# One DMA transpose for two halves of an output block, and a new order for the last pair of products, in a two-layer MLP kernel

## Chip, cores, metric

One core of a Trainium2 chip. The metric is device microseconds (us) of the core, lower is better. Times inside a trace count from the start of its span; the device time is 1.7 to 2.1 us longer than the span.

## The reference

```python
B, S, D, F = 1, 2048, 1024, 3584          # x: bf16 (B,S,D); w1 (D,F); w2 (F,D)
def reference(x, w1, b1, w2, b2):
    y = _layernorm(x, axis=-1)
    h = _gelu(jnp.einsum("bsd,df->bsf", y, w1) + b1)
    return jnp.einsum("bsf,fd->bsd", h, w2) + b2
```

## The kernel before

Both layers are matrix products of the Strassen-Winograd kind, in two levels: seven outer products `p`, each of seven inner products `q`. The second layer computes the output transposed (columns on the partitions), so nearly every output block must be turned before it is stored. A block is 512 tokens by 256 columns, and it comes in two halves `dt` of 128 columns. Blocks of one product are named 11, 12, 21, 22.

A small planner inside the kernel lists all work as tasks, packs the on-chip memory (with a seed), simulates the schedule and emits each engine's instructions in the simulated order. Two things follow. Each engine, and each DMA issue queue, has a fixed list that it works off in order: in the trace of this kernel a weight load leaves at 304.74 us, right behind an output store that had waited until 304.32. And any change of sizes or of the seed packs the memory anew and can reorder instructions far away from the edit.

The parts that matter:

```python
UNIT_LA, IN_LA = (6, 5), 5          # how many products ahead a weight unit is asked for
SEED = 4
# order of the last two outer products: digits are q and dt; "p" marks the outer product before the last
END_ORDER = "11 10 p41 p40 51 p31 61 50 p30 71 60 31 70 30 20 40 41 21"

def finish(dt, i, k, u, v, a, na, bb, nb, name, alone=False, q="SP"):
    o = M.alloc(1024, "o")
    ...
    op("DVE", ..., tensor_tensor(out=o, in0=a, in1=bb, op=add), ...)
    if key not in OT:
        OT[key] = M.alloc(2048, "ot")
    t = OT[key]
    half = view[:, :, dt * P:(dt + 1) * P]
    dma("SP", dma_start_transpose(half, o), ...)         # one transpose per half
    if alone:                store(... half ...)
    elif len(t.cells) == 2:  store(... both halves ...)

def last_ends(dt):           # dt = 1 only: blocks 11 and 21 come "by tokens"
    def turn(u, src, cell):  # the sum so far is split into two fp16 parts, turned by DMA, added again
        ...
        dma("SP", dma_start_transpose(tt, hl), ...)
    def end(u, q):           # last inner product with tokens on the partitions: needs no turn
        prod2(dt, 3)(q, bank, True, tiles)
        op("DVE", ..., add) ; store(...)
...
# a weight load may leave once the product just before the place UNIT_LA places earlier is done (gate)
put(i - (UNIT_LA[0] if p == P_ORDER[0] else UNIT_LA[1]), lambda p=p, q=q: w2_unit(p, q))
```

## Time and profile before

| | before |
|---|---|
| device time, three runs | 338.09 us median (337.15 to 339.26) |
| span of the traced run | 336.6 us |
| tensor engine busy | 327.4 us |
| last matmul ends | 330.43 us |
| tail from there to the end | 6.17 us |
| DMA transposes | 44 (12 of the input, 30 of block halves, 2 double ones of the last blocks) |

The tensor engine is the bound, so the kernel can win only in the few microseconds in which that engine does nothing, or does work that is not needed. Read the view of its waits for the gaps, the end of the chain of waits for the tail, and the timeline with the issue queues (SPq is the sync queue, ACTq the scalar queue) for what fills the tail. The lines stand in the prediction below.

### The profile page before, as it was taken

What the parts mean: (1) busy time and instruction counts of PE and PEld (TensorE: products, weight loads), DVE (VectorE), ACT (ScalarE), POOL (GpSimd) and SP (SyncE); (2) the same over time, 40 slices, a digit from 0 to 9 for tenths busy, and PEclk for the clock granted to TensorE, in tenths of its full rate; (3) what the DMA queues carried; (4) which work ended last, traced back from release to release, by engine and by line L of the source; (5) the groups of instructions that cost most, each with busy time, mean ns of one, the idle gap of its engine ahead of it and who ended that gap; (6) DMA issues with size and microseconds to landing.
All of it is one profiled execution on the core that took longest, in us unless ns stands there. A gap on an engine that the chain in (4) does not pass through costs nothing.

```text
span 336.6 us, 4741 instructions
## 1 busy us (share of the span) xinstructions
PE 327.4 (97%) x1684; PEld 154.7 (46%) x1684; DVE 299.7 (89%) x488; ACT 181.1 (54%) x309; POOL 14.1 (4%) x28
## 2 busy tenths in 40 slices
PE   8999999999999999999999999999999999998992
PEld 6844444444444444444444444444444444443452
DVE  5979999999989969976969998999999998899782
ACT  4697999998776776768666453542112123121220
POOL 2210021103000000000000000000000000000000
PEclk9999999999999999999999999999999999999997
DMA  6998999999997999998775535556799549999998
GB/s 217 322 239 191 277 242 360 237 321 268 291 344 252 344 324 328 340 343 258 238 218 171 164 115 161 163 157 154 213 229 266 151 135 230 190 250 247 283 213 177
DMA packets 122721, 81.00 MB, mean 241 GB/s; under 512 B 36682, under 2 KB 114122, under 8 KB 122698
## 3 DMA queue, kind: packets, MB, share of 16 engines
q1 hardware_dynamic: 119642, 79.59, 87.2%
q10 hardware_dynamic: 3056, 1.11, 1.4%
q8 instruction: 13, 0.21, 0.3%
q14 instruction: 10, 0.08, 0.1%
HBM read 48.70 MB, written 24.38 MB: 217 GB/s over the span
## 4 chain that ended last, share of the span: by engine, by line
PE 88%; DMA 5%; ACT 2%; SPq 1%; DVE 1%; issue 0%; POOLq 0%; POOL 0%
PE ps L921 43%; PE ps L1242 42%; DMA mem<-in_w_dram 3%; PE ps L1315 2%; DMA mem<-w_raw 2%; PE ps L1249 1%; ACT mem L653 1%; ACT mem L826 1%; DVE mem L782 1%; SPq L771 1%; POOLq L571 0%; ACT mem L842 0%; PE ps L704 0%; SPq L643 0%; ACT mem L650 0%
## 5 line engine op out<-in xcount | busy, mean ns | idle before, releaser
L921 PE MATMUL ps<-mem 128*128 128x512 f16 x756 | 164.3, 379 | 0.5 <-DVE mem L782 0.4
L1242 PE MATMUL ps<-mem 128*128 128x512 f16 x672 | 145.9, 379 | 1.2 <-DMA mem<-w_raw 1.2
L921 PEld LDWEIGHTS ps<-mem 128*128 128x128 f16 (+1 forms) x756 | 73.4, 98 | 90.5 <-DVE mem L782 1.5
L842 ACT COPY mem<-ps 128x512 f32<-128x512 f32 x111 | 64.6, 588 | 77.5 <-PE ps L1242 63.7
L1242 PEld LDWEIGHTS ps<-mem 128*128 128x128 f16 (+1 forms) x672 | 65.7, 98 | 80.7 <-DMA mem<-w_raw 1.7
L826 ACT ACTIVATE mem<-ps,b_sb 128x512 f16<-128x512 f32 x112 | 73.5, 692 | 20.7 <-PE ps L921 13.6
L850 DVE TENSOR_TENSOR ps<-ps,mem 128x512 f32<-128x512 f32 x84 | 58.2, 697 | 13.1 <-ACT mem L842 12.2
L1078 DVE TENSOR_TENSOR mem<-mem 128x2048 f16<-128x2048 f16 (+1 forms) x56 | 59.6, 1087 | 2.1 <-PE ps L1242 1.6
L782 DVE TENSOR_TENSOR mem<-mem 128x1024 f16<-128x1024 bf16 (+1 forms) x56 | 37.9, 688 | 2.8 <-DMA mem<-in_w_dram 2.4
L987 DVE TENSOR_TENSOR mem<-mem 128x512 f16<-128x512 f16 (+5 forms) x84 | 37.0, 465 | 1.2 <-DMA mem<-in_w_dram 0.7
L1090 DVE TENSOR_TENSOR mem<-mem 128x2048 f16<-128x2048 f16 (+1 forms) x32 | 33.4, 1089 | 0.0
L833 ACT COPY ps<-ps 128x512 f32<-128x512 f32 x31 | 17.7, 570 | 24.4 <-DVE mem L1139 15.1
L1111 DVE TENSOR_TENSOR mem<-ps,mem 128x512 bf16<-128x512 f32 x22 | 15.0, 688 | 3.3 <-PE ps L1242 3.2
L971 DVE TENSOR_TENSOR mem<-mem 128x2048 f16<-128x2048 bf16 (+1 forms) x16 | 17.4, 1087 | 0.1
L1139 DVE TENSOR_TENSOR mem<-ps,mem 128x512 f32<-128x512 f32 x24 | 16.4, 687 | 1.2 <-PE ps L1242 1.1
L668 DVE BATCH_NORM_STATS2 st_sb<-mem 128x6 f32<-128x512 bf16 x22 | 14.2, 682 | 3.6 <-DMA mem<-in_x_dram 3.6
L748 DVE TENSOR_TENSOR mem<-mem 128x512 f16<-128x512 f16 x32 | 11.9, 419 | 0.2
L674 POOL TENSOR_TENSOR rstd_sb<-vpe_sb,nhalf 128x1 f32<-128x1 f32 x11 | 7.1, 643 | 50.9 <-DVE vpe_sb L671 50.9
L1273 PE MATMUL ps<-ones 128*128 128x128 bf16 (+1 forms) x55 | 6.8, 292 | 1.1 <-POOL ones L609 1.1
L1315 PE MATMUL ps<-mem 128*128 128x128 f16 x112 | 7.4, 219 | 0.3 <-DMA mem<-in_w_dram 0.2
L1228 ACT COPY ps<-b_sb 128x512 f32<-128x512 f32 x6 | 3.5, 590 | 7.4 <-DVE mem L1139 7.2
L677 DVE TENSOR_SCALAR mem<-mem,mv_sb,rstd_sb 128x1024 f16<-128x1024 bf16 (+1 forms) x12 | 6.2, 520 | 1.4 <-POOL rstd_sb L674 1.3
(40 smaller groups left out, 77.4 us busy)
## 6 DMA issues: line engine op xcount, KB each, us to landing
mem<-in_w_dram SPq DMA_DIRECT2D x80, 256.0 KB, 5.0
mem<-w_scr SPq DMA_DIRECT2D x28, 448.0 KB, 3.7
w_scr<-mem SPq DMA_DIRECT2D x21, 512.0 KB, 5.2
w_raw<-mem SPq DMA_DIRECT2D x12, 512.0 KB, 5.6
mem<-w_raw SPq DMA_DIRECT2D x12, 448.0 KB, 3.9
mem<-in_w_dram SPq DMA_DIRECT2D x9, 448.0 KB, 3.8
mem<-in_x_dram SPq DMA_DIRECT2D x15, 256.0 KB, 4.3
out_dram<-mem SPq DMA_DIRECT2D x12, 256.0 KB, 3.4
```

The costliest lines, as they stand in the source:

```text
L782: op("DVE", d_tt(n), lambda e: e.tensor_tensor(out=o[0], in0=a[0], in1=bb[0], op=f), r=[a[1], bb[1]], w=[o[1]], name=f"w1S{k}_{ch}")
L826: op("ACT", A_GELU, lambda e: e.activation(out=dst, in_=banks[bank][:, :], func=ACT.Gelu_apprx_tanh, bias=b1_sb[:, f:f + 1], scale=1.0), r ...
L833: op("ACT", A_CP, lambda e: e.copy(out=banks[dst][:, :], in_=banks[src][:, :]), r=[bank_c[src]], w=[bank_c[dst]], name=name, lat=A_LAT)
L842: op("ACT", A_CP, lambda e: e.copy(out=v16(a, 0, 2048, F32), in_=banks[src][:, :]), r=[bank_c[src]], w=[a.c()], name=name, lat=A_LAT)
L850: op("DVE", D_PS, lambda e: e.tensor_tensor(out=banks[dst][:, :], in0=banks[src][:, :], in1=v16(a, 0, 2048, F32), op=ALU.add), r=[bank_c[s ...
L921: i = e.matmul(banks[bank][:, :], lhsT=lv[:, k, :], rhs=rv[:, k, :], start=(fresh and k == 0), stop=(k == KH - 1), skip_group_check=True)
L971: op("DVE", d_tt(2 * self.n), lambda e: e.tensor_tensor(out=vd, in0=va, in1=vb, op=ALU.subtract), r=self.cells(a) + self.cells(bb), w=self ...
L987: tt = lambda o, a, c: (lambda e: e.tensor_tensor(out=o, in0=a, in1=c, op=ALU.subtract))
L1078: op("DVE", d_tt((k1 - k0) * 512), lambda e, a=a, bb=bb, o=o: e.tensor_tensor(out=o, in0=a[0], in1=bb[0], op=f), r=a[1] + bb[1], w=[t.c(z) ...
L1090: op("DVE", d_tt((k1 - k0) * 512), lambda e, va=va, vb=vb, vd=vd: e.tensor_tensor(out=vd, in0=va, in1=vb, op=f), r=h_cells(b, a, s, k0, k1 ...
L1139: op("DVE", D_PS, lambda e: e.tensor_tensor(out=av(dst), in0=banks[bank][:, :], in1=av(src), op=ALU.add), r=[bank_c[bank], src.c()], w=[ds ...
L1242: i = e.matmul(banks[bank][:, :], lhsT=bv[:, k, :], rhs=av3[:, k, :], start=(fresh and k == 0), stop=(k == KQ - 1), skip_group_check=True)
```

## The change

Intent: fewer and larger transposes on the sync queue, and no transpose late enough to hold up the end. Both halves of a block go into one tile, so that one transpose turns both. In the last pair, blocks 11 of both halves come last, by tokens. Blocks 21, the ones before, are turned by the tensor engine. Weight units of the late products are asked for earlier. The packing seed is another.

```diff
-UNIT_LA, IN_LA = (6, 5), 5
+UNIT_LA, IN_LA = (6, 5, 5, 6, 7, 10, 12), 5
-SEED = 4
+SEED = 2
-END_ORDER = "11 10 p41 p40 51 p31 61 50 p30 71 60 31 70 30 20 40 41 21"
+FIN_DUE, END_DUE = 12.0, 4.0
+END_ORDER = "11 10 p41 50 p40 p31 61 p30 71 60 51 70 30 31 40 41 t3 20 t7 21"
+END_HOW = {(0, 1, 0): "PE", (1, 1, 0): "PE"}
@@ class Wino
-                    elif not self.copied:
+                    elif not self.copied and q in (2, 6):
@@ finish
+                o = M.alloc(2048 if how == "both" else 1024, "o") if new else OT[key]
+                dst = v16(o, 0, 2048, BF16).rearrange("p (t s c) -> p s t c", t=4, s=2)[:, dt] ...
+                if how == "both" and new:
+                    OT[key] = o
+                elif how == "PE":
+                    turned.append((o, o.c(dt), lambda view, cells: store(...)))
+                else:
+                    dma("SP", lambda e: e.dma_start_transpose(v3(t, 0, t.n, n, BF16), v16(o, 0, o.n, BF16)), ...)
+                    store(..., q=q)
@@ new: the turn by the tensor engine ("t3", "t7" in the order)
+            def turn_pe(bank):
+                    for t in range(4):
+                        r = e.transpose(out=pv[:, t, :], in_=v16(o, t * 256, 256, BF16), identity=id16[:, :])
+                op("ACT", 0.45, lambda e: e.copy(out=view, in_=pv), ...)
+                put_out(view, [t.c()])
@@ last_end: now once per half, for block 11 only
-            groups[last].part, groups[last].end = last_ends(1)
+            for g, into in zip(c_seq[-2:], ((0,), (2, 6))):
+                groups[g].part, groups[g].end = last_end(g[1], into)
... (the planner's own estimates of issue times, the identity, bookkeeping: cut)
```

More of the change, by code (lines that the diff above doesn't have):

```diff
@@ L397, in _simulate @@
                     if e in ("SP", "ACTQ", "POOLQ"):
-                        issue = {"Td": 2.0, "To": 1.0}.get(t.name[:2], DMA_ISSUE)
+                        issue = {"Td": 1.6, "To": 1.5}.get(t.name[:2], DMA_ISSUE)
                         free[h] = now + issue
@@ L525 @@
 TE_DUE = 5.0
-FIN_DUE = 12.0
-END_ORDER = "11 10 p41 p40 51 p31 61 50 p30 71 60 31 70 30 20 40 41 21"
+FIN_DUE, END_DUE = 12.0, 4.0
+END_ORDER = "11 10 p41 50 p40 p31 61 p30 71 60 51 70 30 31 40 41 t3 20 t7 21"
+END_HOW = {(0, 1, 0): "PE", (1, 1, 0): "PE"}
 OPA = {1: "A11", 2: "A12", 3: "S4", 4: "A22", 5: "S1", 6: "S2", 7: "S3"}
@@ L582, in bass_standalone__mixer_channel_mlp__prompt_kernel @@
         identb = sb("identb", [NBR, NBR], BF16)
+        id16 = sb("id16", [P, P], BF16)
         NT = ST // P
@@ L615, in build @@
                r=[c_ones], w=[c_idb], name="identb")
+            c_id16 = Cell()
             op("POOL", 0.2, lambda e: e.memset(nhalf[:, :], -0.5), w=[c_nh], name="nhalf")
@@ L873, in step @@
                         if self.last:
-                            self.part["11"](X)
+                            self.part(X)
                     if q == 1:
@@ L877, in step @@
                     elif q == 2 and self.last:
-                        self.end["11"](((Z + 4) % 8, Z))
+                        self.end()
                     elif q == 2:
@@ L902, in step @@
                         add(Z, Z, self.s3, n + "V")
-                        if self.last:
-                            self.part["21"](self.s3)
                         MA.free(self.s3)
                         self.sink["22"](Z)
-                    if q == 4 and self.last:
-                        self.end["21"]((X,))
-                    elif q == 4:
+                    if q == 4:
                         self.prod(4, Y, False)
@@ L1103, in build @@
             OT = {}
-            def finish(dt, i, k, u, v, a, na, bb, nb, name, alone=False, q="SP"):
-                o = M.alloc(1024, "o")
-                wait = 1.0 if q == "ACTQ" else FIN_DUE
-                pr.due = (pr.last_pe, wait)
-                op("DVE", D_PS, lambda e: e.tensor_tensor(out=v16(o, 0, 1024, BF16), in0=a, in1=bb, op=ALU.add),
-                   r=[na, nb], w=[o.c()], name=name, lat=D_PS_LAT)
-                key = (i, k, u, v)
-                if key not in OT:
-                    OT[key] = M.alloc(2048, "ot")
-                t = OT[key]
-                view = v16(t, 0, 2048, BF16).rearrange("p (t c) -> p t c", t=4)
-                half = view[:, :, dt * P:(dt + 1) * P]
-                pr.due = (pr.last_pe, wait + 5.0)
-                dma("SP", lambda e: e.dma_start_transpose(half, v16(o, 0, 1024, BF16)), [o.c()], [t.c(dt)], P * 1024 * 1.3, None, f"To{key}")
-                pr.due = None
-                M.free(o)
-                if alone:
-                    store(i, k, u, v, half, [t.c(dt)], dt * P, P, q=q)
-                    M.free(OT.pop(key))
-                elif len(t.cells) == 2:
-                    store(i, k, u, v, view, [t.c(0), t.c(1)], 0, 2 * P, q=q)
-                    M.free(OT.pop(key))
@@ new lines, in finish @@
+            def finish(dt, i, k, u, v, a, na, bb, nb, name, how="both", q="SP"):
+                key = (i, k, u, v)
+                pr.due = (pr.last_pe, END_DUE if q == "ACTQ" else FIN_DUE)
+                new = key not in OT or how != "both"
+                o = M.alloc(2048 if how == "both" else 1024, "o") if new else OT[key]
+                dst = v16(o, 0, 2048, BF16).rearrange("p (t s c) -> p s t c", t=4, s=2)[:, dt] if how == "both" else \
+                    v16(o, 0, 1024, BF16).rearrange("p (t c) -> p t c", t=4)
+                four = lambda z: z.rearrange("p (t c) -> p t c", t=4)
+                op("DVE", D_PS, lambda e: e.tensor_tensor(out=dst, in0=four(a), in1=four(bb), op=ALU.add), r=[na, nb], w=[o.c(dt)], name=name,
+                   lat=D_PS_LAT)
+                if how == "both" and new:
+                    OT[key] = o
+                elif how == "PE":
+                    turned.append((o, o.c(dt), lambda view, cells: store(i, k, u, v, view, cells, dt * P, P, q=q)))
+                else:
+                    if how == "both":
+                        OT.pop(key)
+                    n = o.n // 256
+                    pr.due = (pr.last_pe, (END_DUE if q == "ACTQ" else FIN_DUE) + 5.0)
+                    t = M.alloc(o.n, "ot")
+                    dma("SP", lambda e: e.dma_start_transpose(v3(t, 0, t.n, n, BF16), v16(o, 0, o.n, BF16)),
+                        [o.c(0), o.c(1)] if how == "both" else [o.c(dt)], [t.c()], P * o.n * 2.2, None, f"To{i}{k}{u}{v}")
+                    M.free(o)
+                    store(i, k, u, v, v3(t, 0, t.n, 4, BF16), [t.c()], 0 if how == "both" else dt * P, 2 * P if how == "both" else P, q=q)
+                    M.free(t)
+                pr.due = None
@@ new lines, in build, with tr @@
+            turned = []
+            def turn_pe(bank):
+                o, cell, put_out = turned.pop(0)
+                pv = banks[bank][:, :].bitcast(BF16)[:, 0:512].rearrange("p (t c) -> p t c", t=4)
+                def tr(e):
+                    for t in range(4):
+                        r = e.transpose(out=pv[:, t, :], in_=v16(o, t * 256, 256, BF16), identity=id16[:, :])
+                    return r
+                op("PE", 4 * MM128, tr, r=[cell, c_id16], w=[bank_c[bank]], name="turn", lat=PE_LAT)
+                M.free(o)
+                t = M.alloc(1024, "ot")
+                view = v3(t, 0, 1024, 4, BF16)
+                op("ACT", 0.45, lambda e: e.copy(out=view, in_=pv), r=[bank_c[bank]], w=[t.c()], name="turned", lat=A_LAT)
+                put_out(view, [t.c()])
+                M.free(t)
@@ L1167, in f @@
                             e6 = E.pop(("6", k))
-                            finish(dt, 0, 1, u, v, banks[bank][:, :], bank_c[bank], av(e6), e6.c(), n, alone=v == 0,
-                                   q="ACTQ")
+                            finish(dt, 0, 1, u, v, banks[bank][:, :], bank_c[bank], av(e6), e6.c(), n, END_HOW.get((dt, u, v), "both"), "ACTQ")
                             M.free(e6)
@@ L1172, in outer_sink, with last_end, part @@
                 return {"11": mk(0, 0), "12": mk(0, 1), "21": mk(1, 0), "22": mk(1, 1)}
-            def last_ends(dt):
-                nat = {}
-                def turn(u, src, cell):
-                    e6 = E.pop(("6", (dt, u, 0)))
-                    n = f"oe{u}"
-                    op("DVE", D_PS, lambda e: e.tensor_tensor(out=av(e6), in0=src, in1=av(e6), op=ALU.add), r=[cell, e6.c()], w=[e6.c()],
-                       name=n + "a", lat=D_PS_LAT)
+            def last_end(dt, into):
+                ee = []
+                def part(bank):
+                    e6 = E.pop(("6", (dt, 0, 0)))
+                    n = f"oe{dt}"
+                    pr.due = (pr.last_pe, 3.0)
+                    op("DVE", D_PS, lambda e: e.tensor_tensor(out=av(e6), in0=banks[bank][:, :], in1=av(e6), op=ALU.add),
+                       r=[bank_c[bank], e6.c()], w=[e6.c(), bank_c[bank]], name=n + "a", lat=D_PS_LAT)
                     hl = M.alloc(2048, "hl")
@@ L1186, in turn @@
                     op("ACT", A_CP, lambda e: e.copy(out=hi, in_=av(e6)), r=[e6.c()], w=[hl.c(0)], name=n + "h", lat=A_LAT)
-                    op("DVE", D_PS, lambda e: e.tensor_tensor(out=lo, in0=av(e6), in1=hi, op=ALU.subtract), r=[e6.c(), hl.c(0)], w=[hl.c(1)],
-                       name=n + "l", lat=D_PS_LAT)
+                    op("DVE", D_PS, lambda e: e.tensor_tensor(out=lo, in0=av(e6), in1=hi, op=ALU.subtract), r=[e6.c(), hl.c(0)],
+                       w=[hl.c(1)], name=n + "l", lat=D_PS_LAT)
@@ L1189, in turn @@
                     M.free(e6)
                     tt = M.alloc(2048, "tt")
-                    dma("SP", lambda e: e.dma_start_transpose(v3(tt, 0, 2048, 8), v16(hl)), [hl.c(0), hl.c(1)], [tt.c()], P * 2048 * 1.3, None,
-                        f"Td{n}")
+                    pr.due = (pr.last_pe, 8.0)
+                    dma("SP", lambda e: e.dma_start_transpose(v3(tt, 0, 2048, 8), v16(hl)), [hl.c(0), hl.c(1)], [tt.c()], P * 2048 * 2.2,
+                        None, f"Td{n}")
+                    pr.due = None
@@ L1193, in turn @@
                     M.free(hl)
-                    ee = nat[u] = M.alloc(2048, "acc")
-                    op("DVE", D_PS, lambda e: e.tensor_tensor(out=av(ee), in0=v16(tt, 0, 1024), in1=v16(tt, 1024, 1024), op=ALU.add),
-                       r=[tt.c()], w=[ee.c()], name=n + "s")
+                    ee.append(M.alloc(2048, "acc"))
+                    op("DVE", D_PS, lambda e: e.tensor_tensor(out=av(ee[0]), in0=v16(tt, 0, 1024), in1=v16(tt, 1024, 1024), op=ALU.add),
+                       r=[tt.c()], w=[ee[0].c()], name=n + "s")
@@ L1197, in turn @@
                     M.free(tt)
-                def end(u, q):
-                    def f(into):
-                        ee = nat.pop(u)
-                        nt = 4 // len(into)
-                        w = nt * P
-                        for z, bank in enumerate(into):
-                            prod2(dt, 3)(q, bank, True, range(z * nt, (z + 1) * nt))
-                            pr.due = (pr.last_pe, 2.0)
-                            o = M.alloc(2 * w, "o")
-                            a, bb, oo = banks[bank][:, 0:w], av(ee)[:, z * w:(z + 1) * w], v16(o, 0, 2 * w, BF16)
-                            op("DVE", 0.08 + w / 960, lambda e, a=a, bb=bb, oo=oo: e.tensor_tensor(out=oo, in0=a, in1=bb, op=ALU.add),
-                               r=[bank_c[bank], ee.c()], w=[o.c()], name=f"oe{u}_{z}", lat=D_PS_LAT)
-                            store(0, 1, u, 0, oo.rearrange("p (t c) -> p t c", t=nt), [o.c()], dt * P, P, z * nt, nt,
-                                  "ACTQ" if z == 0 else "SP")
-                            pr.due = None
-                            M.free(o)
-                        M.free(ee)
-                    return f
@@ L1217, in last_ends, with end @@
-                part = {"11": lambda bank: turn(0, banks[bank][:, :], bank_c[bank]), "21": lambda a: turn(1, av(a), a.c())}
-                return part, {"11": end(0, 2), "21": end(1, 4)}
+                def end():
+                    nt = 4 // len(into)
+                    w = nt * P
+                    for z, bank in enumerate(into):
+                        prod2(dt, 3)(2, bank, True, range(z * nt, (z + 1) * nt))
+                        pr.due = (pr.last_pe, 2.0)
+                        o = M.alloc(2 * w, "o")
+                        a, bb, oo = banks[bank][:, 0:w], av(ee[0])[:, z * w:(z + 1) * w], v16(o, 0, 2 * w, BF16)
+                        op("DVE", 0.08 + w / 960, lambda e, a=a, bb=bb, oo=oo: e.tensor_tensor(out=oo, in0=a, in1=bb, op=ALU.add),
+                           r=[bank_c[bank], ee[0].c()], w=[o.c()], name=f"oe{dt}_{z}", lat=D_PS_LAT)
+                        store(0, 1, 0, 0, oo.rearrange("p (t c) -> p t c", t=nt), [o.c()], dt * P, P, z * nt, nt,
+                              "ACTQ" if dt == 0 or z == 0 else "SP")
+                        pr.due = None
+                        M.free(o)
+                    M.free(ee[0])
@@ L1220, in b2_seeds @@
+                return part, end
             def b2_seeds(dt, h):
@@ L1389, in build @@
                 flat += both(p, 1) + both(prev, 4) + both(p, 5) + both(prev, 3) + both(p, 2, 6, 7)
-            prev, p, last = P_ORDER[-2], P_ORDER[-1], c_seq[-1]
+            prev, p = P_ORDER[-2], P_ORDER[-1]
             for name in END_ORDER.split():
+                if name[0] == "t":
+                    flat.append(((), int(name[1])))
+                    continue
                 flat.append((("c", int(name[-1]), {"p": prev}.get(name[0], p)), int(name[-2])))
@@ L1437, in build @@
                 for q, (dct, key) in {2: (y, (b, 0)), 3: (y, (b, 1)), 4: (T, (b, 4)), 5: (T, (b, 1)), 6: (T, (b, 2))}.items():
-                    put(max(i for i, (gg, qq) in enumerate(flat) if gg[0] == b and qq == q) + 1,
+                    put(max(i for i, (gg, qq) in enumerate(flat) if gg[:1] == (b,) and qq == q) + 1,
                         lambda dct=dct, key=key: M.free(dct.pop(key)))
@@ L1447, in build @@
                 spread([due(f, DUE_W) for f in W2Sums(k0, k1).steps()], pos(lo), pos(hi))
-            lb = {p: max(i for i, (g, q) in enumerate(flat) if g[0] == "c" and g[2] == p and q in (1, 2, 4)) for p in P_ORDER}
+            lb = {p: max(i for i, (g, q) in enumerate(flat) if g[:1] == ("c",) and g[2] == p and q in (1, 2, 4)) for p in P_ORDER}
             put(fC + S1_AT, lambda: out_sum(0, "S1", "A21", "A22", ALU.add, None))
@@ L1466, in build @@
             for i, (g, q) in enumerate(flat):
-                if g[0] != "c" or i > first_use(g[:1] + (1 - g[1],) + g[2:], (q,)):
+                if g[:1] != ("c",) or i > first_use(g[:1] + (1 - g[1],) + g[2:], (q,)):
                     continue
                 p = g[2]
-                put(i - (UNIT_LA[0] if p == P_ORDER[0] else UNIT_LA[1]), lambda p=p, q=q: w2_unit(p, q))
+                put(i - (UNIT_LA[P_ORDER.index(p)]), lambda p=p, q=q: w2_unit(p, q))
                 if q in (5, 6, 7, 3):
@@ L1479, in build @@
             put(fC - 12, b2_diff)
+            put(fC, lambda: op("POOL", 0.35, lambda e: e.affine_select(out=id16[:, :], in_=ones[:, :], pattern=[[-1, P]],
+                                                                       compare_op=ALU.is_equal, fill=0.0, base=0, channel_multiplier=1),
+                               r=[c_ones], w=[c_id16], name="id16"))
             groups = dict(g1)
@@ L1487, in build @@
                 groups[g] = group2(g[1], g[2], g[1])
-            groups[last].last = True
-            groups[last].part, groups[last].end = last_ends(1)
+            for g, into in zip(c_seq[-2:], ((0,), (2, 6))):
+                groups[g].last = True
+                groups[g].part, groups[g].end = last_end(g[1], into)
             for i, (g, q) in enumerate(flat):
@@ L1494, in build @@
                 gate[0] = None
-                groups[g].step(q)
+                if g:
+                    groups[g].step(q)
+                else:
+                    turn_pe(q)
             for i in sorted(at):
```

## The prediction

> **What bounds the kernel now.** I read the page first (who is busy), then the chain of waits, then the waits of the tensor engine, and last the timeline of the final 35 us with both DMA issue queues in it. All times are us from the start of the span.
>
> The page, parts 1 and 5:
>
> ```profile
> span 336.6 us, 4741 instructions
> PE 327.4 (97%) x1684; PEld 154.7 (46%) x1684; DVE 299.7 (89%) x488; ACT 181.1 (54%) x309; POOL 14.1 (4%) x28
> ...
> L1242 PE MATMUL ps<-mem 128*128 128x512 f16 x672 | 145.9, 379 | 1.2 <-DMA mem<-w_raw 1.2
> ```
>
> The tensor engine is busy for 327.4 of 336.6 us, so whatever the change does elsewhere, only about 9.2 us are not matrix work. The next views say where those 9.2 lie. The waits of the tensor engine alone:
>
> ```profile
> PE ps L1242 <- DMA mem<-w_raw: 1.2, 1, 1.2
> PE ps L1273 <- POOL ones L609: 1.1, 1, 1.1
> PE ps L921 <- DVE mem L782: 0.4, 1, 0.4
> PE ps L1315 <- DMA mem<-in_w_dram: 0.2, 1, 0.2
> ```
>
> That is 2.9 us: 1.3 at the head, 0.4 in the first layer, 1.2 late in the second. What is left is after the last matmul. The chain of waits ends so:
>
> ```profile
> 304.74 5.71 DMA mem<-w_raw
> 310.45 0.05 issue
> 310.50 16.79 PE ps L1242 x77
> 327.29 3.14 PE ps L1249 x56
> 330.43 0.02 issue
> 330.45 0.42 DVE mem L1209
> ```
>
> The reader is to see two things: one weight load of 5.71 us that the tensor engine waited for, and a last matmul at 330.43, so a tail of 336.6 - 330.43 = 6.17 us. The timeline of the two stretches shows why. First around the late load:
>
> ```profile
> 301.94 0.50 SPq L1034 DMA_DIRECT2D mem<-w_scr  x1
> 304.32 0.38 SPq L1100 DMA_DIRECT2D out_dram<-mem  x1
> 304.74 0.51 SPq L1031 DMA_DIRECT2D mem<-w_raw  x1
> ```
>
> The sync queue sat from 302.44 to 304.32 in front of an output store. The sync queue's own list of waits puts this kind of store down to waiting for a transpose to land (8 times, up to 1.8 us). The weight load stands right behind it in the same queue; it was issued at 304.74, landed at 310.45, and the matrix engine had run dry at about 309.32. Then the tail:
>
> ```profile
> 326.30 5.29 SPq L1120 DMA_TRANSPOSE mem<-mem  x4
> ...
> 328.88 5.57 ACTq L1100 DMA_DIRECT2D out_dram<-mem  x6
> ...
> 331.64 0.93 SPq L1100 DMA_DIRECT2D out_dram<-mem  x1
> ```
>
> Four transposes leave back to back, 1.32 us each, and with the two before them the queue is full from 323.51 to 331.59. The store of the last product is ready at 330.45 + 0.42 = 330.87 but leaves at 331.64. Later still, the last of the six stores on the scalar queue leaves at 334.06 (a narrower window shows it alone), because it waits for the transpose issued at 330.32; it lands 2.0 us after its issue, at 336.1, and 0.5 us later the span ends. So the last 6 us are set by the sync queue's transposes, not by the last product.
>
> **What the Trainium skill says.** "DMA: Bandwidth & Descriptors", section "Anatomy of one DMA", says that the DMA engines never wait on a semaphore; the wait is done by the issuing sequencer before dispatch. The trace agrees: the load at 304.74 leaves only after the store at 304.32. The same page, section "DMA Transpose (X-bar)", says that two transpose streams from different queues in flight at once can corrupt each other, so all turns stay on one queue, and it names the tensor engine with an identity as the other way. The trace has all 44 DMA transposes on the sync queue. "TensorE: Matmul & The Clock Gate", section "Wait — 56ns, not 53.3ns?", gives 215.7 and 55.6 ns start to start at 512 and 128 columns; the chain has 119.31 us for 553 wide matmuls (215.7 ns) and 3.14 for 56 narrow ones (56.1 ns), which agrees. No page that I found states what a transpose costs to issue; I use the trace.
>
> **The change part by part.**
>
> 1. Merging the two halves of a block. Before there are 30 block transposes (128 x 512 elements) of 1.24 us median issue and 3.9 us to landing. After it, blocks of the four earlier kinds need one each instead of two (24 become 12), and of the last product two merged ones remain of six, so 14. In the trace a transpose of twice the width costs hardly more to issue: the two double ones near the end took 1.23 and 1.49 us, and landed after 5.7 and 3.7 us. Saved: 16 x 1.24 = 20 us of the sync queue, and nearly none of it on the path by itself. No vector work is saved: the adds stay, with another output layout.
>
> 2. Weight units of the last two products are asked for 10 and 12 products ahead, not 5. One product is 7 matmuls, 1.51 us. The late load's gate so comes 5 x 1.51 = 7.5 us earlier, against a lateness of 1.18 us. I count the whole gap as gone: -1.18.
>
> 3. Both "11" blocks are now the two by tokens at the end (28 narrow matmuls each). Before it was 11 and 21 of one half. So the count of token work is the same, 56 x 0.056 = 3.14 us, and the wide products stay 16. Nothing gained, nothing lost: 0.
>
> 4. Both "21" blocks are turned by the tensor engine, 4 transposes each between the last products: 8 x 0.056 = +0.45 on the tensor engine, if the vector engine's add is done in time. The first is asked for after another product of 1.51 us; the add needs some 0.25 + 0.69, so it is. The scalar engine's two copies of about 0.5 us lie where it has nothing else.
>
> 5. The tail. With parts 2 and 4 the last matmul ends at 330.43 - 1.18 + 0.45 = 329.70. The last half block needs 0.02 + 0.42 for the add, then a store. The sync queue has no transposes left by then (the last, of blocks 12, comes after a product that ends some 6.6 us before the end), so it leaves at 330.2. A store of 64 KB lands 3.3 us after issue on this queue before; then 0.5 to the end: 334.0. The tail is then 4.3 instead of 6.17: -1.85.
>
> Against that the merged transpose of blocks 12: the product ends at about 323.05, add to 324.1, transpose landed at 4.7 us (median of the two double ones) 328.8, store landing 3.1 later, 331.9; at 5.7 us it would be 332.9. Both are before 333.5, so the last product sets the end, with 0.6 to 1.6 us to spare.
>
> Sum: -1.18 + 0.45 - 1.85 = -2.6. The memory is packed anew (another seed, larger output tiles, longer prefetch), and that draws the small waits of 20 to 310 us anew. Before has only 0.4 of them beside the one removed, which is nearly as good as it gets, so I put +0.5 there, a judgement and not a reading. Result -2.1: span 334.5, time 338.09 - 2.1 = 336.0.
>
> **The rivals.**
>
> - A new wait takes the place of the old one. For: the weight units stay allocated longer, the packing is another, and each load is issued in order on one queue; the vector engine is at 100% from 300 to 310.5 already, so a late sum has nowhere to go. Against: the DMA share from 180 to 300 us is 51 to 81%, with room. It would cost 1 to 2 us: 337 to 338.
> - The tail stays set by a DMA. For: a merged transpose starts only when its later half is there, and stores on the scalar queue are in order behind the one that waits for it, with the turned copies on the same engine. Against: the 0.6 to 1.6 us of slack above. It would give back about 1: 337.
> - The turn stalls the tensor engine. For: product, add, turn, copy is a chain over three engines, and the vector engine's order is fixed beforehand; each turn could wait 0.5 to 0.8. Then +1 to +1.5: 337 to 337.5.
> - The gain is larger because the sync queue of the whole second layer is relieved. Against: the tensor engine has no other wait from 95.25 on, so there is nothing to gain there.
>
> **Range and chances.** If all goes as computed without the allowance, 335.5; with one rival whole, 337 to 337.5; with two, 338. The three runs before spread from 337.15 to 339.26, so a median can be off by some 0.5. I take 336.0, and 334.4 to 337.9 for 8 in 10. Faster by over 2% would need 331.3, that is 6.8 us of at most 9.2 that are not matrix work, of which a store's landing alone is 3.3: chance 0.02. Slower by over 2% would need a new stall of 9 us: 0.02. Within 2%: 0.96.
>
> **What would show each step right or wrong.** Part 1: 28 transposes in all instead of 44, the merged at about 1.25 us of issue (wrong if it is near 2.5). Part 2: no wait of the tensor engine for a weight load after 180 us; any there is the first rival. Part 4: 8 narrow transposes on the tensor engine, no idle time before them. Part 5: from the last matmul to the end 4.3 us, and the last store on the sync queue within 0.2 us of the last add; if a store on the scalar queue lands last, the second rival holds. The prediction is wrong as a whole if the busy time of the tensor engine grows by more than 0.5 us or its idle time between 20 and 310 us exceeds 1.5.

## The result

| | before | after |
|---|---|---|
| device time, six runs each on one chip | 337.67 us median (336.74 to 339.26) | 333.88 us median (333.2 to 334.65) |
| ratio, with 95% interval | | 0.9887 (0.9859 to 0.9914) |
| span of the traced run | 336.6 us | 332.7 us |
| last matmul ends | 330.43 us | 329.63 us |
| tail | 6.17 us | 3.07 us |

A ratio is the mean time of one kernel's fast runs over that of the other's fast runs of the same rounds, so it is not quite the ratio of the medians. The change is faster by 1.1%, within the 2% that I gave 0.96, but the time lies 0.5 us below my range. Fewer transposes were issued: 28, of which the 14 output ones took a median of 1.27 us to issue and 4.4 to land.

The page of the changed kernel, parts 1 and 5:

```profile
span 332.7 us, 4721 instructions
PE 328.1 (99%) x1692; PEld 156.2 (47%) x1692; DVE 299.3 (90%) x488; ACT 181.8 (55%) x311; POOL 13.6 (4%) x29
...
L1262 PE MATMUL ps<-mem 128*128 128x512 f16 x672 | 145.7, 379 | 0.0
```

The tensor engine does a little more work than before (328.1 against 327.4) and yet the span is 3.9 us shorter, so all of the gain is idle time (of the 0.7 us more, 2 x 0.22 are the turns shown below, and 0.2 lie in the first 20 us, 18.84 against 18.64 busy); the second layer's wait of 1.2 is now 0.0. The waits of the tensor engine (what waited, for what: us in total, times, longest):

```profile
PE ps L1293 <- POOL ones L611: 1.1, 1, 1.1
PE ps L920 <- DVE mem L751: 0.4, 1, 0.4
```

The late weight load is gone from the list. The granted clock is no rival: its mean was 0.994 in the trace before and 1.000 after, but before it stands at 1.00 until 332 us and falls (to 0.72, then 0.50) only after the last matmul. The end of the chain of waits (start, us, what):

```profile
326.04 0.22 PE ps L1142 x4
326.26 1.56 PE ps L1269 x28
327.83 0.22 PE ps L1142 x4
328.05 1.58 PE ps L1269 x28
329.63 0.02 issue
329.65 0.42 DVE mem L1231
```

The turns on the tensor engine (L1142) cost 2 x 0.22 us with no idle time before them, as worked out beforehand, and the last matmul ends at 329.63 where the prediction had 329.70. (That it fits to 0.07 us is partly luck: in a second trace of the same kernel, after_again below, it ends at 328.93.) Then the issue queues of the tail; the last line is from a narrower window, which shows the second of the two stores alone:

```profile
317.10 7.91 SPq L1126 DMA_TRANSPOSE mem<-mem  x3
325.05 5.43 SPq L1099 DMA_DIRECT2D out_dram<-mem  x2
...
330.10 0.37 SPq L1099 DMA_DIRECT2D out_dram<-mem  x1
```

The last transpose has left by 325.01, and the last store leaves at 330.10, 0.03 us after the last add (329.65 + 0.42). Before it stood 0.77 us behind transposes. The span then ends 2.60 us after that issue.

That is where the prediction breaks: it allowed 3.3 + 0.5 = 3.8 us for this last piece. The DMA view of the last microseconds (how many, KB each, median us from issue to landing), before:

```profile
out_dram<-mem ACTq DMA_DIRECT2D x3, 128.0 KB, 3.1
...
out_dram<-mem ACTq DMA_DIRECT2D x1, 64.0 KB, 3.5
out_dram<-mem SPq DMA_DIRECT2D x1, 64.0 KB, 3.3
```

and after:

```profile
out_dram<-mem ACTq DMA_DIRECT2D x3, 128.0 KB, 2.3
out_dram<-mem ACTq DMA_DIRECT2D x1, 64.0 KB, 1.8
```

The same stores land 0.8 to 1.7 us sooner. For the very last store of the changed kernel the view gives no landing; the 2.60 us to the end bound it. So the view does not show whether this store or the scalar queue's last one (issued at 329.75, landed after 2.2) came in last.

### The profile page after: what moved, and what is told of

It is laid out like the page before. It is cut to its first block, busy times and chain, and to the rows that moved or that the text cites. A ratio compares the mean times of both kernels' runs of the same rounds, so it can differ in the third digit from the quotient of the medians.

```text
span 332.7 us, 4721 instructions
## 1 busy us (share of the span) xinstructions
PE 328.1 (99%) x1692; PEld 156.2 (47%) x1692; DVE 299.3 (90%) x488; ACT 181.8 (55%) x311; POOL 13.6 (4%) x29
## 4 chain that ended last, share of the span: by engine, by line
PE 90%; SPq 5%; DMA 4%; DVE 0%; issue 0%
PE ps L920 45%; PE ps L1262 44%; SPq L774 3%; DMA mem<-mem 2%; DMA mem<-in_w_dram 1%; SPq L646 1%; PE ps L1269 1%; DVE mem L751 0%; SPq L1310 0%; PE ps L1142 0%; DVE mem L1231 0%; SPq L643 0%; SPq L1311 0%
## 5 line engine op out<-in xcount | busy, mean ns | idle before, releaser
L1293 PE MATMUL ps<-ones 128*128 128x128 bf16 (+1 forms) x55 | 7.7, 322 | 1.1 <-POOL ones L611 1.1
L653 ACT ACTIVATE mem<-mem 128x1024 f16<-128x1024 bf16 x5 | 5.3, 1069 | 3.6 <-DMA mem<-in_x_dram 3.6
```

## The experiments

Theory A: the gain is two separate things, a late weight load (1.2 us) and a shorter tail (3.1 us), less 0.45 us of turning. Inside the tail, theory F: stores land late because transposes load the DMA engines. The rivals: B, everything comes from a crowded sync queue; C and H, the new packing of the memory; D, merging does not pay by itself.

The last matmul, the tail and the waits are of the traced run, the rest of the timed runs. A tail is good to some 0.05 us, since the span is read to 0.1. "Weight wait" is the wait of the tensor engine for a second-layer weight load; "other waits" are those of 0.4 us or more after the first microseconds.

| run | last matmul | tail | weight wait | other waits | median us | ratio to before (95%) |
|---|---|---|---|---|---|---|
| before_look1 | 329.52 | 6.28 | 0.7 | none | (337.58) | |
| before_look2 | 330.23 | 5.97 | 1.1 | 0.5 | (337.91) | |
| after_again | 328.93 | 2.97 | none | none | 333.54 | 0.9896 (0.9871 to 0.9921) |
| e1_prefetch_only | 329.17 | 5.53 | none | 0.4 | 336.97 | 1.0003 (0.9976 to 1.0030) |
| e2_merge_only | 328.08 | 7.22 | none | none | 337.78 | 1.0016 (0.9998 to 1.0034) |
| e3_after_old_prefetch | 329.89 | 3.61 | none | 0.6 | 336.39 | 0.9979 (0.9958 to 0.9999) |
| e4_after_halves_apart | 329.93 | 3.77 | none | 0.6 | 335.17 | 0.9940 (0.9921 to 0.9958) |
| e5_after_no_pe_turn | 328.43 | 4.17 | none | none | 334.86 | 0.9942 (0.9918 to 0.9967) |
| e6_after_one_pe_turn | 330.97 | 3.63 | none | 1.4, 0.6 | 336.28 | 0.9975 (0.9953 to 0.9998) |
| e7_after_seed4 | 329.56 | 3.04 | none | 0.7 | 334.39 | 0.9917 (0.9896 to 0.9937) |
| e8_after_loaded_tail | 334.77 | 6.63 | none | 2.8, 0.6 | 342.20 | 1.0150 (1.0115 to 1.0186) |
| e9_before_seed2 | 330.12 | 5.98 | none | 1.2 | 338.00 | 1.0028 (1.0004 to 1.0051) |
| e10_after_seed1 | 328.66 | 3.04 | none | none | 333.67 | 0.9897 (0.9868 to 0.9926) |
| e11_after_seed3 | 331.37 | 3.03 | none | 1.7, 0.6 | 336.09 | 0.9959 (0.9929 to 0.9988) |
| e12_one_pe_turn_seed4 | 331.92 | 3.78 | none | 1.8, 0.6 (in two) | 336.99 | 0.9992 (0.9964 to 1.0019) |

All gave the right result. One of the six runs of e11 (340.71 us) was slow and is not in its ratio. Runs of different chips are compared by their ratios to the kernel before.

### Is the weight wait a standing cost? (before_look1, before_look2)

No edit: the kernel before, looked at again on another chip.

> The kernel before, looked at again on another chip, because the prefetch alone (e1) removed the wait in its trace and yet timed no better. If the 1.2 us wait for a weight load is a standing cost, it is here again (1 us or more), the last matmul at about 330.4 and the tail near 6.2 us. If it was the luck of one trace, there is no such wait, the last matmul comes at 329.3 or so, and the tail is 5.5 to 6.2.

> A second look at the kernel before on the same chip, as the first: a standing wait shows in both, a chance one in none or one; the tail should be 5.5 to 6.2 us in both.

The wait lists of the tensor engine, first look, then second:

```profile
PE ps L1242 <- DMA mem<-w_raw: 0.7, 1, 0.7
```

```profile
PE ps L1242 <- DMA mem<-w_raw: 1.1, 1, 1.1
```

It is standing, 0.7 to 1.2 us in three traces (look 1 falls short of the 1 us that I had asked for), and so is the tail of about 6 us.

### The look-ahead alone (e1_prefetch_only)

```diff
-UNIT_LA, IN_LA = (6, 5), 5
+UNIT_LA, IN_LA = (6, 5, 5, 6, 7, 10, 12), 5
```

> The kernel before, with only the longer look-ahead for the second layer's weight loads (10 and 12 products for the last two, not 5). Theory A (the 3.8 us gained are two separate things: 1.2 us of a late weight load, and 3.1 us of a shorter tail, less 0.45 us of turning on the tensor engine): the wait of 1.2 us for a weight load is gone, the tail after the last matmul stays near 6.2 us, so 1.2 us faster than before: about 336.5 us. Rival B (the sync queue's transposes are the cause of both, the look-ahead only moves the loads to another place in the same crowded queue): a wait of 0.5 us or more stays, no faster than before by more than 0.7 us. Rival C (the new packing of the memory did it): anything, and the waits appear elsewhere.

In the trace the weight wait is gone and the last matmul comes earlier, as theory A says; the tail stays long. The issue queues of its last microseconds show why (the second and the last line are from narrower windows):

```profile
323.61 5.59 SPq L1120 DMA_TRANSPOSE mem<-mem  x4
327.59 1.61 SPq L1120 DMA_TRANSPOSE mem<-mem  x1
329.65 0.52 SPq L1100 DMA_DIRECT2D out_dram<-mem  x1
332.30 0.38 ACTq L1100 DMA_DIRECT2D out_dram<-mem  x1
```

The sync queue does not hold up its last store here: it leaves 0.03 us after the last add (329.20 + 0.42). The end hangs on the scalar queue. The last of the four transposes, issued at 327.59, lands after 4.7 us, at 332.3; the scalar queue's last store leaves only then, 3.1 us after the last matmul, and lands after 2.0. The timed runs, however, gained nothing (1.0003). Their spans range from 334.4 to 337.1 us, and only the traced one (334.7) can be looked into. So the look-ahead is enough to remove the wait in a trace, but I can't show that it gains time by itself: of rival B's two signs the time is there (no more than 0.7 us faster) and the wait is not.

### Merging alone (e2_merge_only)

```diff
-                o = M.alloc(1024, "o")
+                o = M.alloc(1024 if alone else 2048, "o") if new else OT[key]
...
-                dma("SP", ... transpose(half, o) ...)             # per half
+                dma("SP", ... transpose(whole tile, o) ...)       # once both halves are there
```

> The kernel before, with only the merging of two halves into one transpose (44 become 31 or so; the last pair's order and token products as before). Theory A: the late load has less in front of it, the 1.2 us wait falls to between 0 and 1.2; the tail loses two of its eight transposes but the last two still come after the last wide products, so the tail falls by 0.5 to 1.5 us; 336 to 337 us. Rival B (the crowded sync queue is the cause of everything): wait gone and tail at 3.5 us or less, 334 us. Rival D (merging does not pay, since the merged transpose waits for its later half and lands later): tail as long as before or longer, 337.7 or more.

Theory A fails, since the tail did not shrink, and what rival D forecast came: a longer tail and 337.78 us. The weight wait is gone here too, and the last matmul comes at 328.08, earlier than in the changed kernel. But the tail grew to 7.22 us. The end of its chain of waits:

```profile
325.19 4.60 DMA mem<-mem
329.79 0.02 issue
329.81 0.70 DVE mem L1198
```

A transpose issued at 325.19 landed only at 329.79, and the vector engine waited for it with the sum that the last token product needs; the matmuls had been over for 1.7 us. On the sync queue that transpose left behind two merged ones (322.53 to 325.14); that it was the waiting for a later half that made it late, as D has it, is not shown. Merging without the new order takes away the tensor engine's wait and makes a new one behind it: the time is the same (1.0016).

### The change without the look-ahead (e3_after_old_prefetch)

```diff
-UNIT_LA, IN_LA = (6, 5, 5, 6, 7, 10, 12), 5
+UNIT_LA, IN_LA = (6, 5, 5, 5, 5, 5, 5), 5
```

> The changed kernel with the look-ahead of before for the weight loads (5 products for all but the first). Theory A in its strict form (the look-ahead removed the wait): a wait of the tensor engine for a weight load of about 1 us comes back, 334.9 us. Rival B (merging emptied the queue in front of the load, the look-ahead does nothing): no wait, 333.9 us, the tail at 3.1 us in both.

No wait for a weight load came back, so theory A in its strict form falls: with the transposes merged, the look-ahead is not needed for that. Yet it was 0.8% slower than the changed kernel (0.9979 against 0.9896), some 2.8 us, which is most of the gain and more than rival B allows. The trace shows 0.6 us of waiting for a vector add before the last products, some 0.5 us in the first microseconds, and a tail of 3.61. That is about 1.7 us; the rest of the loss stays unexplained, as the traced run was the fastest of six. And the look-ahead came out together with a new packing, so which of the two costs this is not shown.

### The change with the halves turned apart (e4_after_halves_apart)

```diff
-                o = M.alloc(2048 if how == "both" else 1024, "o") if new else OT[key]
+                o = M.alloc(1024, "o")
...
+                    half = view[:, :, dt * P:(dt + 1) * P]
+                    dma("SP", lambda e: e.dma_start_transpose(half, v16(o, 0, 1024, BF16)), ...)
```

> The changed kernel with each half turned by a transpose of its own again (14 more transposes on the sync queue; order, look-ahead and turning on the tensor engine as changed). Theory A (the tail is short because the last transposes now come 6 us before the end, not because they are merged): last matmul at about 329.6 us still, tail 3.1 to 3.7 us, at most 0.6 us slower than the changed kernel: 333.9 to 334.5. Rival B (merging is the lever): a weight wait returns or the tail grows by over 1 us: 335 or more.

By the ratios (0.9940 against 0.9887 and 0.9896) it is 0.4 to 0.5% slower than the changed kernel, some 1.6 us: above theory A's 0.6 us. Its 335.17 us is in rival B's range, but neither of B's signs is there: no weight wait returned, and the tail grew by 0.7 us, not by over 1. Over half of the gain is there without merging, since the tail is 3.77 us and not 6; of what is missing, the trace has 0.6 us as a wait for a vector add and 0.7 us in the tail. So with order, turns and look-ahead changed the tail is short even without merging, and with merging it is 0.7 us shorter still.

### No turn on the tensor engine (e5_after_no_pe_turn)

```diff
-END_ORDER = "... 30 31 40 41 t3 20 t7 21"
-END_HOW = {(0, 1, 0): "PE", (1, 1, 0): "PE"}
+END_ORDER = "... 30 31 40 41 20 21"
+END_HOW = {}
```

> The changed kernel, with blocks 21 turned by one merged DMA transpose instead of by the tensor engine. Theory A (turning on the tensor engine buys a tail without late transposes): the last matmul comes 0.45 us earlier, at 329.2, but the transpose of 21 is issued at about 327.1, lands at 331 and its store at 333.5, and the last store of the product lands later too (3 us and more instead of 2.1) because the 16 DMA engines are busy with the transpose: span 334.0, 1.3 us slower than the changed kernel. Rival E (the turning is only a cost): 0.45 us faster, 332.2.

after_again: 333.54 against 334.86. The last matmul came 0.50 us earlier (0.45 expected), and the tail grew by 1.2 us. The sync queue:

```profile
321.35 5.92 SPq L1126 DMA_TRANSPOSE mem<-mem  x3
328.91 0.37 SPq L1099 DMA_DIRECT2D out_dram<-mem  x1
```

The last of the transposes now leaves at 326.05. The two 64 KB stores land after 2.3 us instead of 1.8 and 2.1 (the 2.1 is from e10, the changed kernel with another seed, where the view gives it), less than the 3 that I expected, and the scalar queue issues its last store until 329.73, 1.30 us after the last matmul; in the changed kernel that is 330.25, 0.62 after. So the turn buys 1.2 us of tail for 0.50 us of matmul time. The spans of the two traces differ by 0.7 us (332.6 against 331.9); the rest of the 1.3 us lies outside the span and is not explained.

### What makes the last store land late (e8_after_loaded_tail)

```diff
+    for _ in range(2 if dt == 0 else 1 - z):       # three in all
+        junk = M.alloc(2048, "tt")
+        dma("SP", lambda e, ...: e.dma_start_transpose(v3(junk, 0, 2048, 8), src[:, 0:1024]), ..., extra=(pr.last_pe,))
...
-                              "ACTQ" if dt == 0 or z == 0 else "SP")
+                              "ACTQ")
```

> The changed kernel with three useless DMA transposes of 256 KB thrown in on the sync queue during the last two products by tokens, into memory that nobody reads, and with both last half stores on the scalar queue, so that no store stands behind a transpose in a queue. The result stays right. Theory F (a store of 64 KB lands after 3.3 to 3.5 us in the kernel before and after 1.8 to 2.1 in the changed one because transposes load the 16 DMA engines): the two 64 KB stores land after 3 us or more, the stores of 128 KB after 3 or more. Rival G (it was only the order in the sync queue that made the store late): they land after 1.8 to 2.3 us as in the changed kernel. The span also ends on the useless transposes, some 333 to 334 us, which says nothing.

The DMA view of its last microseconds, to be laid beside the two in the section on the result:

```profile
out_dram<-mem ACTq DMA_DIRECT2D x3, 128.0 KB, 4.3
...
out_dram<-mem ACTq DMA_DIRECT2D x2, 64.0 KB, 5.0
```

The stores leave on the scalar queue, where no transpose stands, and they land after 5.0 and 4.3 us instead of 1.8 and 2.3. (Of the two 64 KB stores the trace gives a landing for one.) So rival G falls, and theory F holds for this load: with three more transposes of 256 KB in flight, stores land late though none stands behind a transpose. It does not hold for every store beside a transpose. In e5 the transpose issued at 326.05 landed after 3.1 us, and a 128 KB store issued meanwhile, at 327.62, landed after 2.1; in e2 a 64 KB store issued at 330.99, 0.2 us after a transpose's issue had ended, landed after 1.7. How much traffic it takes was not measured, nor whether ordinary copies of the same bytes would do the same. The Trainium skill has the ground for it in "DMA: Bandwidth & Descriptors", section "Issuing engines are not separate DMA queues": DMAs from the scalar and the sync engine run on the same 16 DMA engines and interleave. This run agrees, and gives the price for its load. The time of the run itself (342.20 us; its span is 341.4, where 333 to 334 was expected) says nothing: its last microseconds are those of the useless transposes and of the stores that they slow, and 3.4 us of waits came in elsewhere.

### The packing (e7, e9, e10, e11) and one turn instead of two (e6, e12)

Edits: `SEED` alone in e7 (4), e10 (1) and e11 (3) of the changed kernel and in e9 (2) of the kernel before. In e6 and e12:

```diff
-END_ORDER = "... 40 41 t3 20 t7 21"
-END_HOW = {(0, 1, 0): "PE", (1, 1, 0): "PE"}
+END_ORDER = "... 40 41 20 t7 21"
+END_HOW = {(0, 1, 0): "DMA", (1, 1, 0): "PE"}
```

> The changed kernel itself once more, on this call's chip, to compare the next ones with it. Theory A: the last matmul at 329.4 to 329.9 us, no wait for a weight load, a tail of 3.0 to 3.2 us, a ratio to before of 0.986 to 0.991. If the small waits of the middle are luck of one trace, the ratio would lie above 0.992.

> The changed kernel with the packing seed of the kernel before (4). Theory H (the packing of the memory draws small waits anew, and the seed was part of what was chosen): the tail stays 3.0 to 3.3 us, but waits of the tensor engine of 0.5 to 3 us appear between 20 and 325 us: 334 to 336.5. If the packing does not matter: within 0.3 us of the changed kernel, 333.5 to 333.9.

> The kernel before with the packing seed of the changed one (2), nothing else. Theory C (the new seed alone explains a good part of the 3.8 us): 334 to 335.5 us. Theory A (the tail is the larger part and does not hang on the packing): tail 5.5 us or more, between 336.5 and 339 us.

> The changed kernel with packing seed 1. Theory H (the packing draws small waits; the changed kernel's draw is a good one): waits of the tensor engine between 20 and 326 us of 0.5 us or more, tail 3.0 to 3.3 us, 334 to 336 us, a ratio to before of 0.991 to 0.998. If the draw is typical: 0.5 us or less of waits, a ratio of 0.987 to 0.990.

> The changed kernel with packing seed 3. As seed 1: theory H 0.991 to 0.998 with waits of 0.5 us or more; if the draw of the changed kernel is typical, 0.987 to 0.990. The tail 3.0 to 3.3 us in any case.

> A candidate: the changed kernel with only the second block 21 turned by the tensor engine; the first, 1.5 us earlier, by a DMA transpose of its own. Theory A: the last matmul 0.22 us earlier (329.4); the transpose is issued at about 325.5 and lands near 329.5, its store near 332, so it just fits: 0 to 0.3 us faster than the changed kernel. If the transpose slows the last stores: 0.3 to 1 us slower.

> e6 (one block turned by the tensor engine, the other by a transpose of its own) with packing seed 4 instead of 2. If e6 lost 2.7 us to its packing (1.4 us waiting for a weight load in the first layer): that wait is gone or another size, and the ratio to before falls to 0.990 to 0.995. If the single turn itself costs (a tail of 3.6 instead of 3.0, and 0.6 us of waiting for an add before the last products): these two are here again, together 1.2 us, and it does not beat the changed kernel.

The changed kernel once more (after_again) gave the ratio that was expected, but its last matmul came at 328.93, earlier than the 329.4 to 329.9 expected. The four seeds of the changed kernel have the same tail (2.97 to 3.07 us) and differ in their waits. The worst, e11 (wait list of the tensor engine):

```profile
PE ps L920 <- DVE mem L785: 1.7, 1, 1.7
...
PE ps L1262 <- DVE ps L853: 0.6, 1, 0.6
```

Seeds 2 and 1 are clean and equal (0.9896 and 0.9897), seed 4 loses a little (0.9917), seed 3 more (0.9959). So the packing can take back over half of the gain, as theory H says for seed 3, but not for seed 1. In the other direction, the new seed given to the kernel before (e9) does nothing for it (1.0028): its weight wait is gone and 1.2 us of another wait took its place. Rival C falls.

The candidate with one turn does not beat the changed kernel with either seed; with seed 2 it is 0.8% slower (0.9975 against 0.9896), more than either of its forecasts. e6 had a tail of 3.63 us and waits of 1.4 and 0.6 us; with seed 4 the 1.4 was gone, but the wait for the vector add grew from 0.6 to 1.8 us and the tail stayed at 3.78. In e6 two sums of the vector engine (2.08 us from 317.10) stand in front of the add that the tensor engine waits for; in the changed kernel they don't. Why the planner orders them so I did not follow. None of these variants was found faster than the changed kernel.

## Why the prediction was wrong

It forecast -2.1 us for a time of 336.0; measured were -3.8 us and 333.88. By its own steps:

1. **Merging: right in count and cost.** 28 transposes, 1.27 us of issue each. "Nearly none of it on the path by itself" is right as to the total time (e2), though not as to the reason: e2 lost the weight wait and gained another behind it.
2. **Look-ahead, -1.18: the size is right, the credit is not.** The wait is gone; but merging removes it as well (e2, e3), and so did a new seed (e9). Any one is enough, so no part owns it. In time, the look-ahead added alone gained nothing (e1), and taking it out of the changed kernel lost 0.8% without a weight wait (e3).
3. **Token products, 0: right.**
4. **Turns, +0.45: right.** Measured 2 x 0.22, no stall. With points 2 to 4 the last matmul was put at 329.70 and came at 329.63 (328.93 in the second trace, so part of this fit is luck).
5. **The tail, -1.85: the direction right, the size wrong, and this is the step that failed.** The issue of the last store came at 330.10 where I had "about 330.2". The mis-sized term is "3.3 us after issue on this queue before; then 0.5": 3.8 us, where 2.60 was measured. I took the landing time of a store from a tail full of transposes and used it for a tail from which I had just removed them. The number that would have warned me stood in my own text: the very last store before, issued when the transposes were through, landed after 2.0 us. e8 shows that transposes in flight can do this (1.8 us without, 5.0 with three more of them); that it takes transposes, and not any traffic of their size, is not shown.
6. **The allowance for new packing, +0.5: not needed in this draw.** The changed kernel lost 0.4 us in one trace and none in another. As a mean over packings it was not foolish (0, 0, 0.7 and 2.3 us for seeds 1, 2, 4 and 3), but it should have widened the range below as much as above.

The base moved too: the six runs beside the changed kernel have a median of 337.67, not 338.09. The miss of 2.1 us (336.0 against 333.88) is therefore about 0.4 of base, 1.2 of landing and 0.5 of allowance.

One of the signs that the prediction named for being wrong as a whole did come: the tensor engine's busy time grew by 0.7 us (limit 0.5). It was no sign of a wrong path, since 0.45 of it was forecast and 0.2 lies in the first 20 us; the limit was set too close to the forecast. And one reading in it is off: the DMA share "from 180 to 300 us" was not 51 to 81%. In stretches of 30 us it was 52, 62, 81 and 90%, so there was less room than that at the end.

Of the rivals, "a new wait takes the place of the old one" did not happen in the changed kernel but in e3, e4, e6, e7, e11 and e12; "the tail stays set by a DMA" happened in e5, where the scalar queue's last store had to wait for the late transpose.

What stays open: what the new order gives by itself, and what the planner's changed estimates and due times (the part cut from the diff) give, as neither was run alone; why e1 gained in its trace and not in its timed runs; the rest of the loss of e3; whether it takes transposes to slow a store; and why the device time exceeds the span by 2.1 us in some kernels (e3, e5, e9) and 1.7 to 1.9 in others.

## What to carry to other kernels

A landing time read from a trace is valid for the traffic in which it was read; if a change removes that traffic, size the term with the quietest transfer of the same kind in the trace (here the 2.0 us of the last store before would have given 2.5 for the last piece, and 2.60 was measured). At the end of a kernel, look at the issue queues after the last matmul: half a microsecond of extra work on the bound engine can buy more than a microsecond of tail when it takes a DMA off the end. And test the parts of a combined change both ways. Added alone to the kernel before, the look-ahead and the merging gained nothing that could be measured (1.0003 and 1.0016), and merging turned one wait into another; taken out of the changed kernel they cost 0.8% and 0.4%, each with a packing of its own.

## What the Trainium skill lacked or had wrong

- "DMA: Bandwidth & Descriptors" says that DMAs from different issuing engines interleave on the same 16 engines, but I found no figure for what transposes in flight do to small stores: 64 KB stores landed after 1.8 us (after), 3.3 to 3.5 (before, between transposes) and 5.0 (e8, three more transposes), but after 1.7 in e2 with the last transposes still under way.
- The same page gives what a transpose costs its issuing sequencer only as cycle counts, in a table that sets "previous generations" beside trn3 (the prediction missed that table); on this chip an on-chip transpose of 128 x 512 two-byte elements took a median of 1.24 us on the sync queue and one of twice the width 1.27, so by these medians the issue cost hardly depends on the width. No page that I read says that.
- Nothing was found wrong: the matmul spacings (215.7 ns at 512 columns, 56.1 at 128) and the waits on the issuing queue agree with the pages cited.
